# Seven small edits to a sparse attention and tanh-shrink kernel: crossbar turns for half of q, shared threshold biases, a deeper score pipeline, work moved to GpSimd

## The chip, the cores and the metric

One core of a Trainium2 chip. The metric is device microseconds of one execution, the median of several; a ratio is always the mean time of one kernel's fast runs over the mean time of the other's fast runs of the same rounds, so it is not quite the ratio of the medians quoted beside it. A difference between two edited kernels is the difference of their ratios times 552 us, the time of the kernel before; each ratio is known to about 0.15%, which is 0.8 us, so a difference of two is known to about 1 us. Stage lengths come from one profiled execution of each kernel.

## The reference

Eight batches of eight heads, 576 rows of 64. Scores are thresholded at the row's maximum less tau, then softmax; the result, 4608 rows of 512, goes through two matrices with h - tanh(h) between them.

```python
scores = scale * np.matmul(q, k.transpose(0, 1, 3, 2))
thresh = np.max(scores, axis=-1, keepdims=True) - tau
scores = np.where(scores >= thresh, scores, -1e9)
attn = softmax(scores)                      # cut
x = heads_side_by_side(np.matmul(attn, v))  # cut
h = x @ w_in
return (h - np.tanh(h)) @ w_out
```

## The kernel before

A turn is a transpose of a block of 128 columns, by TensorE into PSUM or by the crossbar, the transposing path of the DMA queue (`dma_start_transpose`), into SBUF. The depth is the number of slots by which the scores run ahead (`AHEAD`). In the views PE is TensorE, PEld its weight loads, DVE VectorE, ACT ScalarE, POOL GpSimd and SPq the DMA queue of SyncE.

Two heads make a pair; 32 pairs of nine tiles of 128 rows (kinds A, B, and M for the two heads' last 64 rows). Each tile goes through the engines slot by slot: TensorE scores, VectorE scale and row maximum (`sc`, `mx`), VectorE bias (`nb` = tau - max), ScalarE mask (`z`), a turn of the mask (`psZ` by TensorE in pairs 0 to 7, `zT` by the crossbar later), ScalarE exponential (`pT`), TensorE times v (`psO`). The hidden layer of the previous batch (`psH`, `psY`) is fed into the slots from pair 4 on. GpSimd splits the next pairs' q and k into high and low halves.

```python
NPE = 2 * HPAIR * TPP          # masks turned on TensorE: pairs 0 to 7
AHEAD = 7                      # scores run 7 slots ahead of the exponentials
MASK = 5                       # masks 5 slots ahead
zt_pool = pool("zt", 4)        # crossbar-turned masks in flight
ps_big = pool("ps_big", 2, space=PSUM)   # scores and turns of q, k
ps_y = pool("ps_y", 1, space=PSUM)       # turned masks, then output blocks
# ... cut ...
def split(p, t):                               # GpSimd
    x = hl_pool.tile([P, TPP, D], F32, name="xs", tag="xs")
    nc.gpsimd.tensor_scalar(out=x, in0=r, scalar1=QKSC, ...)
    nc.gpsimd.tensor_copy(out=hl[:, :, 0, :], in_=x)
    nc.gpsimd.tensor_tensor(out=hl[:, :, 1, :], in0=x, in1=hl[:, :, 0, :], op=ALU.subtract)

def turn(p, t):                                # nine 128x128 turns, one copy
    ps = ps_big.tile([P, W], FP16, name=f"ps_{t}", tag="big")
    for c in range(TPP): turn_chunk(...)
    nc.vector.tensor_copy(out=m, in_=ps)
# ... cut ...
def scores(i):
    # ... matmuls into ps ...
    mx = st_pool.tile([P, 1], F32, name="mx", tag="mx")
    nc.vector.tensor_scalar(out=sc, in0=ps[:, lo : lo + S], scalar1=SC, scalar2=None,
                            op0=ALU.mult, op1=ALU.max, accum_out=mx)

def shift(i):                                  # one bias for each tile
    nb = st_pool.tile([P, 1], F32, name="nb", tag="nb")
    nc.vector.tensor_scalar(out=nb, in0=mx, scalar1=-1.0, scalar2=tau,
                            op0=ALU.mult, op1=ALU.add)

def kink(i):                                   # the mask
    nc.scalar.activation(out=z, in_=sc, func=ACT.Prelu, bias=nb, scale=1.0, alpha=STEEP)
# ... cut ...
for s in range(-AHEAD, NTILE + LAG + 3):       # one slot
    shift(s + AHEAD - 1); scores(s + AHEAD)
    kink(s + MASK); bend(); weights(s)         # + hidden-layer steps
    attend(s - LAG)                            # + loads, splits, turns of later pairs
```

## Time and profile before

| | |
|---|---|
| time, median of 3 runs | 552.6 us (551.52 to 552.71) |
| span in the profile | 549.4 us, granted clock 0.999 |
| busy | TensorE 521.8, VectorE 444.1, ScalarE 443.3, GpSimd 286.5 us |

In a timeline or a table of stretches the first numbers are start and length in us. In a line of groups, the numbers after "x" and the count are total busy us and mean ns of one instruction; behind the second bar stands how long the engine was idle just before these instructions, and who ended most of that.

### The profile page before, as it was taken

The page shows a single profiled execution, that of the slowest core. Times are in us where ns is not written, and L with a number is a line of the kernel's source. Part 1 is how long each engine was busy: PE and PEld are TensorE (multiplying, and loading weights), DVE is VectorE, ACT ScalarE, POOL GpSimd, SP SyncE. Part 2 cuts the span into 40 slices and gives each one's busy share as a digit, 9 for nine tenths or more (in the row PEclk, how much of TensorE's full clock was granted, in tenths as well). Part 3 has the DMA queues.
Part 4 walks back from the last instruction along what each step waited for, and adds up shares of the span by engine and source line. Part 5 has one row for each costly group of instructions (what it writes and reads, how often), then busy time and mean ns, then how long its engine had stood idle before and what let it go on. Part 6 is the DMA issues. An engine that isn't in the chain of part 4 may idle for free.

```text
span 549.4 us, 13518 instructions
## 1 busy us (share of the span) xinstructions
PE 521.8 (95%) x4954; PEld 302.4 (55%) x4954; DVE 444.1 (81%) x1349; ACT 443.3 (81%) x640; POOL 286.5 (52%) x372
## 2 busy tenths in 40 slices
PE   5888999999999999999999999999999999999996
PEld 2566666665555555555555555555555555444442
DVE  5888988898988999898889898898989888544430
ACT  3999999899899898989888988989898989533320
POOL 6788977666556666556555655666665620000000
PEclk9999999999999999999999999999999999999999
DMA  6755644437879888889977798877878966310103
GB/s 168 216 183 146 205 125 145 128 74 157 161 153 172 178 181 160 169 171 170 186 174 173 165 182 164 167 180 179 163 169 171 185 87 144 66 39 38 40 38 78
DMA packets 183011, 80.33 MB, mean 146 GB/s; under 512 B 150688, under 2 KB 175264, under 8 KB 182944
## 3 DMA queue, kind: packets, MB, share of 16 engines
q1 hardware_dynamic: 182512, 79.17, 65.0%
q8 instruction: 39, 0.64, 0.5%
q10 hardware_dynamic: 432, 0.30, 0.2%
q14 instruction: 28, 0.23, 0.2%
HBM read 37.75 MB, written 9.44 MB: 86 GB/s over the span
## 4 chain that ended last, share of the span: by engine, by line
PE 72%; DVE 16%; ACT 8%; issue 2%; DMA 1%; SPq 0%; ACTq 0%; DVEq 0%
PE psY L470 20%; PE psH L444 18%; PE psS L292 15%; DVE sc L298 6%; PE psO L389 5%; ACT pT L352 4%; PE psS L282 3%; ACT z L324 3%; DVE g L463 3%; PE psHt L444 3%; PE ps_q L221 2%; PE ps_k L221 2%; PE psZ L343 2%; DVE yo L479 1%; DVE kT L233 1%
## 5 line engine op out<-in xcount | busy, mean ns | idle before, releaser
L298 DVE TENSOR_SCALAR_CACHE_REDUCE sc<-psS 128x576 f32<-128x576 f32 x288 | 216.3, 751 | 19.8 <-PE psS L282 12.5
L324 ACT ACTIVATE z<-sc,nb 128x576 bf16<-128x576 f32 x256 | 195.7, 769 | 14.3 <-DVE nb L307 13.4
L470 PE MATMUL psY<-w_out_sb,g 128*128 128x512 bf16 x576 | 145.4, 379 | 0.0
L360 ACT ACTIVATE pT<-zT 128x1152 f16<-128x1152 bf16 (+1 forms) x120 | 127.8, 1065 | 0.0
L444 PE MATMUL psH<-xT,w_in_sb 128*128 128x512 bf16 x480 | 124.0, 379 | 0.3
L292 PE MATMUL psS<-kT,qT 128*128 128x512 f16 (+1 forms) x512 | 105.2, 287 | 10.1 <-DVE nb L307 7.6
L292 PEld LDWEIGHTS <-qT 128*128 128x128 f16 x1024 | 75.5, 98 | 68.1 <-issue 15.9
L237 POOL COPY kS<-kT 64x1152 f16<-64x1152 f16 x31 | 35.3, 1140 | 141.4 <-DVE nb L307 141.4
L463 DVE SCALAR_TENSOR_TENSOR g<-th,psH 128x512 bf16<-128x512 f32 x128 | 87.4, 683 | 22.0 <-ACT th L457 22.0
L292 PE MATMUL psS<-kS,qT 128*128 128x512 f16 x496 | 101.4, 286 | 0.0
L457 ACT ACTIVATE th<-psH 128x512 f32<-128x512 f32 x128 | 74.7, 584 | 17.8 <-PE psH L444 17.6
L470 PEld LDWEIGHTS <-g 128*128 128x128 bf16 x576 | 49.6, 98 | 57.7 <-issue 2.6
L444 PEld LDWEIGHTS <-w_in_sb 128*128 128x128 bf16 x576 | 49.3, 98 | 55.0 <-issue 2.7
L389 PEld LDWEIGHTS <-pT 128*128 128x128 f16 x1280 | 55.6, 98 | 24.3 <-ACT pT L360 2.1
L389 PE MATMUL psO<-vb,pT 128*128 128x65 bf16 x1280 | 61.2, 193 | 0.6 <-ACT pT L360 0.6
L352 ACT ACTIVATE pT<-psZ 128x640 f16<-128x640 bf16 (+1 forms) x72 | 47.2, 656 | 6.9 <-PE psZ L343 6.2
L307 DVE TENSOR_SCALAR nb<-mx 128x1 f32<-128x1 f32 x288 | 42.6, 148 | 3.4
L324 ACT ACTIVATE zm<-sc,nb 128x576 bf16<-128x576 f32 x32 | 24.8, 774 | 23.1 <-DVE nb L307 23.1
L183 POOL TENSOR_TENSOR qhl<-xs,qhl 128x576 f16<-128x576 f32 x31 | 39.7, 1280 | 2.6
L183 POOL TENSOR_TENSOR khl<-xs,khl 128x576 f16<-128x576 f32 x31 | 39.7, 1279 | 2.6
L238 POOL COPY kS<-kT 64x1152 f16<-64x1152 f16 x31 | 35.4, 1142 | 1.3
L343 PE MATMUL psZ<-ident_bf,z 128*128 128x128 bf16 x288 | 26.5, 219 | 4.5 <-ACT pT L352 4.3
(72 smaller groups left out, 561.6 us busy)
## 6 DMA issues: line engine op xcount, KB each, us to landing
vraw<-in_v_dram SPq DMA_DIRECT2D x32, 256.0 KB, 3.5
out_dram<-yo SPq DMA_DIRECT2D x32, 256.0 KB, 2.6
kraw<-in_k_dram SPq DMA_DIRECT2D x31, 256.0 KB, 3.1
qraw<-in_q_dram SPq DMA_DIRECT2D x31, 256.0 KB, 3.2
wt<-in_moe_w_in_dram SPq DMA_DIRECT2D x8, 512.0 KB, 4.4
wt<-in_moe_w_out_dram SPq DMA_DIRECT2D x8, 512.0 KB, 3.9
vraw<-in_v_dram SPq DMA_DIRECT2D x64, 32.0 KB, 2.9
zT<-z SPq DMA_TRANSPOSE x96, 3.3
```

The lines of the kernel that those rows point to most:

```text
L183: nc.gpsimd.tensor_tensor(out=hl[:, :, 1, :], in0=x, in1=hl[:, :, 0, :], op=ALU.subtract)
L292: nc.tensor.matmul(out=ps[:, dst], lhsT=lhs, rhs=kk[:, src], start=(n == 0), stop=(n == 1),)
L298: nc.vector.tensor_scalar(out=sc, in0=ps[:, lo : lo + S], scalar1=SC, scalar2=None, op0=ALU.mult, op1=ALU.max, accum_out=mx,)
L307: nc.vector.tensor_scalar(out=nb, in0=mx, scalar1=-1.0, scalar2=tau, op0=ALU.mult, op1=ALU.add)
L324: nc.scalar.activation(out=z, in_=sc, func=ACT.Prelu, bias=nb, scale=1.0, alpha=STEEP)
L352: nc.scalar.activation(out=pt[:, off * P : (off + n) * P], in_=ps[:, 0 : n * P], func=ACT.Exp)
L360: nc.scalar.activation(out=pt[:, 0 : n * P], in_=zts.pop(i)[:, 0:n, :], func=ACT.Exp)
L389: nc.tensor.matmul(out=po[:, (j - 1 - 5 * hh) + ab, :], lhsT=pt[:, blk * P : (blk + 1) * P], rhs=vb[:, hh, c, :], start=(n == 0), stop=(n ...
L444: nc.tensor.matmul(out=ps, lhsT=w_in_sb[:, c, n * P : (n + 1) * P], rhs=xs[m][:, c, :] if m < B else xR[:, c, :, :], start=(c == 0), stop= ...
L457: nc.scalar.activation(out=th, in_=ps, func=ACT.Tanh)
L463: nc.vector.scalar_tensor_tensor(out=gs[m][:, n, :], in0=th, scalar=-1.0, in1=ps, op0=ALU.mult, op1=ALU.add,)
L470: nc.tensor.matmul(out=ps, lhsT=gs[m][:, n, ms * P : (ms + 1) * P], rhs=w_out_sb[:, n, :], start=(n == 0), stop=(n == DF_C - 1),)
```

## The change

Its intent: relieve TensorE, which is the bound from pair 8 on, by turning q of every second later pair and some masks of pairs 4 to 7 in the crossbar; save VectorE 128 tiny bias instructions by computing the biases of an A and a B tile together; give the pipeline one slot and the turned masks two buffers more; put part of the first split on GpSimd; shorten the tail.

```diff
-    NPE = 2 * HPAIR * TPP
+    def on_pe(i):
+        p, j = divmod(i, TPP)
+        return p < HPAIR or p < 2 * HPAIR and j in (0, 1, 4, 5, 6)
-    AHEAD = 7
+    AHEAD = 8
-    zt_pool = pool("zt", 4)
+    zt_pool = pool("zt", 6)
 # split: x in place; split_first, second half: three GpSimd instructions
 # in place of one on ScalarE and one on VectorE, issued before the loop
+    def q_by_dma(p):
+        return p >= 2 * HPAIR and p % 2 == 1
     def turn(p, t):
+        if t == "q" and q_by_dma(p):
+            nc.sync.dma_start_transpose(out=m..., in_=hl...)
+            return
     def scores(i):
-        mx = st_pool.tile([P, 1], F32, name="mx", tag="mx")
+        if kind(j) == "B":
+            mx = mxs[i] = mxs.pop(i - 1)
+        else:
+            mx = mxs[i] = st_pool.tile([P, 2], F32, name="mx", tag="mx")
     def shift(i):
+        if kd == "A":
+            return
+        n = 2 if kd == "B" else 1
         nc.vector.tensor_scalar(
-            out=nb, in0=mx, scalar1=-1.0, scalar2=tau, op0=ALU.mult, op1=ALU.add
+            out=nb[:, 0:n], in0=mx[:, 0:n], scalar1=-1.0, scalar2=tau,
+            op0=ALU.mult, op1=ALU.add,
         )
     def weights(i):
-            ps = ps_y.tile([P, 5 * P], BF16, name="psZ", tag="y")
+            pl, tag = (ps_h, "h") if i % 2 and i < HPAIR * TPP else (ps_y, "y")
+            ps = pl.tile([P, 5 * P], BF16, name="psZ", tag=tag)
 # v: last rows loaded once, GpSimd writes both copies
 # layers: three quarters of an output block one stage earlier,
 # the last block in two halves of 256 columns, stored from two queues
 # (cut: order of the first masks, slots in which turns and hidden-layer steps
# are issued, where the rows of a crossbar-turned q lie, one-time constants)
```

## The prediction

> **What bounds the kernel now.** I read the page first (TensorE busy 95% of 549.4 us, VectorE and ScalarE 81% each, the clock full throughout), then cut the span where the work changes and read the busy times stage by stage. Columns: stretch, length, busy us (instructions) of PE, PEld, DVE, ACT, POOL, granted clock, DMA share, GB/s.
>
> ```profile
> 0.00:9.20 9.20, 3.13 (x25) 2.02 (x26) 2.98 (x24) 3.63 (x7) 4.17 (x17) 1.00 0.64 174
> 9.20:20.30 11.10, 9.40 (x83) 5.23 (x82) 10.17 (x31) 7.45 (x12) 8.60 (x11) 1.00 0.76 226
> 20.30:68.80 48.50, 43.10 (x595) 31.38 (x595) 42.50 (x144) 45.86 (x74) 43.58 (x54) 1.00 0.57 175
> 68.80:127.50 58.70, 54.85 (x655) 36.41 (x652) 51.09 (x163) 53.71 (x88) 42.72 (x54) 1.00 0.42 119
> 127.50:472.80 345.30, 340.63 (x3258) 195.04 (x3257) 309.10 (x950) 308.79 (x422) 187.44 (x240) 1.00 0.82 166
> 472.80:544.80 72.00, 70.69 (x347) 32.28 (x345) 28.25 (x44) 23.23 (x39) 0.00 (x0) 1.00 0.13 45
> 544.80:549.40 4.60, 0.00 (x0) 0.00 (x0) 0.00 (x0) 0.59 (x1) 0.00 (x0) 0.83 0.25 57
> ```
>
> Seven stages, three kinds of limit. From 127.5 us to 544.8 us TensorE is busy 98.6% and 98.2%: it is the bound, and only less work on it, or fewer holes in it, helps. Between 20.3 and 127.5 us (head pairs 1 to 8 by their first score tile) no engine is full: four engines stand at 86 to 95% and wait for each other. The ends, 9.2 us before the first scaled score and 4.6 us after the last matmul, are latency.
>
> A busy TensorE need not be a full one, so I looked at starts in the timeline. This is the second stage of that kind, pairs 1 to 4, around the q turn of a pair:
>
> ```profile
> 39.86 0.60 ACT L352 ACTIVATE pT<-psZ 128x512 f16<-128x512 bf16 x1 [0.52 <-PE psZ L343]
> 39.99 0.41 PE L292 MATMUL psS<-kT,qT 128*128 128x512 f16 x2 [0.55 <-DVE nb L307]
> ...
> 40.51 0.44 PE L343 MATMUL psZ<-ident_bf,z 128*128 128x128 bf16 x5
> ...
> 41.09 0.67 PE L221 MATMUL ps_q<-ident_f,qhl 128*128 128x128 f16 x9
> ...
> 41.80 0.76 DVE L233 COPY qT<-ps_q 128x1152 f16<-128x1152 f16 x1 [0.22 <-PE ps_q L221]
> ```
>
> ScalarE waits for the turned mask (psZ, one buffer, so a turn must wait for the exponential before it), TensorE waits for VectorE to release a score buffer, VectorE waits for the q turn. A ring of three engines, none full. Summing starts in 20.3 to 68.8 us, I find about 9 us of holes on TensorE: 5.4 behind the score matmuls, 3.9 behind psZ. In a later period of four pairs (231.3 to 290.4 us, 59.17 us; the pattern repeats to 0.1 us), psY and psH matmuls start every 216 ns, and I find only 1.4 us of holes, 0.7 of it in the four slots that have no hidden-layer work.
>
> These groups give the unit costs:
>
> ```profile
> L307 DVE TENSOR_SCALAR nb<-mx 128x1 f32<-128x1 f32 x288 | 42.6, 148 | 3.4
> L233 DVE COPY qT<-ps_q 128x1152 f16<-128x1152 f16 x31 | 23.4, 756 | 7.7 <-PE ps_q L221 7.7
> L343 PE MATMUL psZ<-ident_bf,z 128*128 128x128 bf16 x288 | 26.5, 219 | 4.5 <-ACT pT L352 4.3
> L221 PE MATMUL ps_q<-ident_f,qhl 128*128 128x128 f16 x288 | 21.8, 220 | 0.5 <-DVE sc L298 0.3 <-DVE nb L307 0.2
> ```
>
> Finally the waits of the DMA queue on SyncE, and the transposes' landing:
>
> ```profile
> SPq L332 <- ACT pT L360: 64.1, 37, 3.9
> ```
>
> ```profile
> zT<-z SPq DMA_TRANSPOSE x96, 3.3
> ```
>
> 37 transposes stand in the queue until an exponential gives a turned tile back: four such tiles are too few. It costs nothing yet: from issue to the exponential I count 4.06 us at least, 7.4 in the median, and the exponentials from turned tiles have 0.0 us of idle before them.
>
> **What the Trainium skill says.** "TensorE: Matmul & The Clock Gate", "Wait — 56ns, not 53.3ns?": warm matmuls of 128 columns start 55.6 ns apart, of 512 columns 215.7 ns. The trace agrees: nine turns take 0.67 us (8 x 55.6 + 220), and the long matmuls start 216 ns apart. So a turn of 128 columns is worth 56 ns, not the 220 ns of its row. "VectorE: DVE Perf Modes", "The three transpose paths": a crossbar transpose lands in SBUF, a TensorE one in PSUM; here the PSUM route costs the 756 ns copy as well. "Perfetto Trace Analysis", "Identifying the Most-Contended Engine": matmul busy share is no measure of headroom, and DMA occupancy misleads with 16 engines. I therefore judge the DMA side (0.82 busy) by landings against deadlines, not by its share. Same page, "Matmuls": independent groups should rotate through PSUM banks, which is what the second psZ buffer does; the psZ waits agree.
>
> **The change, part by part.**
> 1. q of pairs 9, 11, ..., 31 by crossbar: 12 pairs x 9 turns x 55.6 ns = 6.0 us off TensorE, all in the TensorE-bound stage. 12 copies x about 0.67 us start to start (8.0 us) off VectorE, 12 fewer claims on the two big PSUM buffers. It adds 12 transposes of 1.3 us issue to SyncE; the second copy of v's last rows, 31 later issues of about 0.6 us, is gone, so the queue is not longer. In the period I measured, packets take 51.4 us of the 16 engines; 18 more blocks of 128 packets at 24 ns add 3.5, the lost v rows give 0.8 back: about 54 of 58 us. Six turned tiles let transposes start up to 3.9 us earlier. Holes: I take 0.3 us off each of about six periods. Together -7.5 us (6.0 + 1.8, rounded down).
> 2. In pairs 4 to 7, 16 of 36 mask tiles (j = 2, 3, 7, 8) go by crossbar: 4 x 2 x 9 turns x 55.6 ns = 4.0 us off TensorE, and eight fewer exponentials on ScalarE (1150 against 596 + 704 ns). Start sums for this stage give floors near 52 us for TensorE, 51 for ScalarE, 53 for VectorE of 58.7. After: about 48, 51, 51. With the ring slackened by parts 2 and 3, I expect 54: -4.5 us.
> 3. Threshold biases: one instruction for tiles A and B, 160 in place of 288. 128 x 148 ns = 19 us in the rows, but these overlap: start to start about 60 to 110 ns each, so some 10 us of VectorE, none of it on the path of the TensorE-bound stage. In pairs 1 to 4 it works with the alternating psZ buffer. Floors there: VectorE 43 to about 41.5, ScalarE 43.6, but GpSimd about 45.6 (9.1 us a pair plus nine 1.0 us weight casts). GpSimd is the new limit: 48.5 becomes 46: -2.5 us.
> 4. Start: the second half of the first split moves to GpSimd, earlier; VectorE loses 1.3 us of split in a stretch where it is 92% busy, and the first masks, at 13.5 us now, can come before 12. GpSimd gets about 2.6 us more before the next pair's split. -1.5 us.
> 5. The deeper pipeline: one more slot with scores but no weights at the start, one with weights but no scores at the end: +0.5 us.
> 6. Tail: three quarters of an output block (2.6 us) move from the tail into the period that starts at pair 8, TensorE-bound in both places: 0. The last block in two halves: a copy of 256 columns in place of the 0.59 us one, the last two stores on two queues in place of two issues in a row: -1.0 us.
> 7. Split in place and the v rows' source: memory and traffic, about 0.
>
> Sum: -7.5 - 4.5 - 2.5 - 1.5 + 0.5 - 1.0 = -16.5 us. 552.6 - 16.5 = **536 us**.
>
> **The rivals.** (a) The crossbar becomes the bound. For it: windows of 13.7 and 16.1 us already show shares of 0.94 and 0.93, one exponential came 4.06 us after its issue, and landings reach 4.6 us. Against: no exponential waits today, and the buffers that held transposes back are added. If so, parts 1 and 2 give back most: 543 to 550 us. (b) GpSimd paces the first 127 us: it is 90% busy in pairs 1 to 4 and gets more at the start; then the swapped k comes late and parts 2 to 4 give 3 us rather than 8.5: 541 us. (c) The ring opens more than I think and the holes of the TensorE stage close too (4.2 us of score waits over all periods): 529 us. (d) VectorE takes over from TensorE: it needs about 54.5 us of a 59.2 us period by starts, about 51.5 after, against 57.5 to 58 for TensorE: unlikely.
>
> **Range and chances.** The certain part is turns removed from a full TensorE (6 us); the early stages are guesses about a ring and carry most of the spread; (a) makes the slow side longer. 8 times in 10 between **529 and 544 us**. Faster by 2% means under 541.5 us: **0.79**; within 2% **0.19**; slower **0.02**.
>
> **What would show it.** Right: a period of four pairs of about 58 us in place of 59.17 (the one from pair 8 longer by 2.6 us), 180 turns fewer on TensorE (108 of q, 72 of psZ), 160 bias instructions, the queue's wait for the exponentials nearly gone, exponentials still without idle time, pairs 1 to 4 near 46 us with GpSimd the fullest, first masks before 12 us, 3.6 us after the last matmul. Wrong: idle time before the exponentials from turned tiles or before scores that wait for q (rival a), score matmuls waiting for the swapped k (rival b), or a period that stays at 59 us although the turns are gone.

## The result, and the profile after

The changed kernel takes 545.05 us (544.2 to 545.15, 4 runs), the kernel before 552.06 us on the same chip: ratio 0.9872, 95% interval 0.9851 to 0.9893. That is 7.0 us, where 16.5 us were predicted; 545.05 us lies outside the range of 529 to 544 us. It is 1.3% faster, within the 2% that count as the same, to which the prediction gave 0.19.

To see where, I cut the span by work done rather than by the clock: at the first scaled score, at the end of attention of pairs 0, 3, 7 and 31 (the start of the reciprocal of the pair's second head), and at the last matmul. The last column is a kernel from the experiments below, with one part of the change mended.

| stage, us | before | after | with two narrow biases |
|---|---|---|---|
| to the first scaled score | 9.2 | 8.5 | 9.3 |
| to the end of pair 0 | 22.9 | 22.5 | 21.3 |
| pairs 1 to 3 | 36.1 | 36.4 | 34.7 |
| pairs 4 to 7 | 58.7 | 56.8 | 56.2 |
| pairs 8 to 31 | 347.7 | 347.1 | 343.5 |
| tail to the last matmul | 70.2 | 67.7 | 67.7 |
| after it | 4.6 | 3.9 | 3.9 |

The first rows are rough: the first scaled score comes between 8.5 and 9.5 us in profiles of kernels that start alike. The tail is as predicted (2.6 us of it now lie in the stage of pairs 8 to 31). The loss is in the middle: pairs 1 to 3 gained nothing, and pairs 8 to 31, where 6 us of turns left a full TensorE and 2.6 us of output block came in, gained 0.6 us, where they should have gained about 4.9. These are the middle stretches of the changed kernel; columns as in the prediction's table (the tail is cut at 539.2 us, 0.1 us behind the last matmul).

```profile
31.06:67.42 36.36, 31.43 (x450) 23.05 (x448) 34.50 (x97) 34.41 (x57) 34.54 (x42) 1.00 0.61 184
67.42:124.20 56.78, 49.05 (x562) 31.43 (x570) 52.81 (x144) 52.85 (x80) 43.17 (x54) 1.00 0.77 165
124.20:471.32 347.12, 337.29 (x3135) 188.97 (x3188) 309.97 (x851) 308.79 (x424) 186.66 (x239) 1.00 0.88 173
471.32:539.20 67.88, 66.66 (x323) 31.80 (x329) 26.93 (x42) 22.41 (x38) 0.00 (x0) 1.00 0.14 44
```

TensorE is busy less while the stage is as long, and VectorE, which lost over a hundred instructions, is as busy as before (in the stage of pairs 8 to 31: 309.97 us; before, 311 us by the same cut) or, in pairs 1 to 3, busier (34.50 against 32.1 us). Note that this trace lacks 68 matmul records of 4790 (the weight loads, 4790, are complete), all of the hidden layer, one about every 6 us, so its TensorE busy time is a little low. The groups say what became of VectorE:

```profile
L337 DVE TENSOR_SCALAR nb<-mx 128x2 f32<-128x2 f32 x128 | 44.4, 347 | 2.5
L337 DVE TENSOR_SCALAR nb<-mx 128x1 f32<-128x1 f32 x32 | 4.6, 144 | 0.0
L357 ACT ACTIVATE z<-sc,nb 128x576 bf16<-128x576 f32 x256 | 194.2, 771 | 21.9 <-DVE nb L337 21.3
L394 ACT ACTIVATE pT<-zT 128x1152 f16<-128x1152 bf16 x104 | 119.9, 1153 | 0.0
L227 PE MATMUL ps_q<-ident_f,qhl 128*128 128x128 f16 x180 | 14.0, 223 | 1.5 <-POOL qhl L180 1.1 <-DVE sc L323 0.3
```

The bias of one column takes 144 ns, as all 288 did before (148 ns). The bias of two columns takes 347 ns in the mean. 160 instructions now cost VectorE 49.1 us where 288 cost 42.6. ScalarE's masks wait 21.3 us for a bias, but that is no loss: in the kernel before they waited 13.4 us (A and B tiles) and 23.1 us (M tiles). The exponentials from turned tiles wait for nothing (0.0), and TensorE waited for a q turned by the crossbar once, 1.5 us, so the crossbar is not what holds the kernel back, and 108 of 288 q turns are gone, as planned. One long bias, in the timeline of all engines:

```profile
216.29 0.41 PE L313 MATMUL psS<-kT,qT 128*128 128x512 f16 x2
216.32 1.28 POOL L180 TENSOR_TENSOR qhl<-qraw,qhl 128x576 f16<-128x576 f32 x1
216.47 0.08 DVE L323 DVE_READ_ACCUMULATOR sc<-psS 128x1 f32 x1
216.54 0.41 PE L313 MATMUL psS<-kS,qT 128*128 128x512 f16 x2
216.56 0.60 ACT L491 ACTIVATE th<-psH 128x512 f32<-128x512 f32 x1
216.59 1.03 DVE L337 TENSOR_SCALAR nb<-mx 128x2 f32<-128x2 f32 x1
...
217.05 1.16 ACT L394 ACTIVATE pT<-zT 128x1152 f16<-128x1152 bf16 x1
...
217.54 0.74 DVE L323 TENSOR_SCALAR_CACHE_REDUCE sc<-psS 128x576 f32<-128x576 f32 x1
```

GpSimd starts a subtraction at 216.32 that ends at 217.60. VectorE starts its bias at 216.59; it ends at 217.62. The next scaled score, which frees a PSUM buffer for TensorE, can only start at 217.54, although its scores were complete at 216.95. Of the 57 two-column biases over 250 ns in this trace, all 57 end within 40 ns of the end of a GpSimd instruction (28 of them of a subtraction); of the 42 that start while GpSimd is idle, none is over 170 ns. The wait does not show as idle time of VectorE, since it lies inside the instruction's own record.

That became theory W: **a bias of more than one column waits until the GpSimd instruction in flight is done**. The Trainium skill has this on a page that I had not read for the prediction, "SBUF — State Buffer", "Who interferes with whom": VectorE's second pair of SBUF ports is GpSimd's only pair; a tensor_scalar can enter a 2-port mode, and then whoever comes second fully blocks for the whole instruction of the other. Its rivals: R, the missing gain lies in the ring of the early stages and in the crossbar, and the long biases are a symptom; later, D, the eighth slot costs in itself.

### The profile page after: what moved, and what is told of

Its sections match the earlier page's. It is cut to its first block, busy times and chain, and to the rows that moved or that the text cites. A ratio compares the mean times of both kernels' runs of the same rounds, so it can differ in the third digit from the quotient of the medians.

```text
span 542.9 us, 12962 instructions
## 1 busy us (share of the span) xinstructions
PE 507.5 (93%) x4722; PEld 290.3 (53%) x4790; DVE 447.1 (82%) x1196; ACT 439.3 (81%) x630; POOL 290.7 (54%) x390
## 4 chain that ended last, share of the span: by engine, by line
PE 67%; DVE 19%; POOL 6%; ACT 4%; issue 3%; DMA 0%; ACTq 0%; SPq 0%; DVEq 0%; POOLq 0%
PE psY L504 19%; PE psH L478 17%; PE psS L313 14%; DVE sc L323 9%; PE psO L423 5%; DVE g L497 3%; PE psS L303 3%; PE ps_k L227 3%; PE psHt L478 3%; DVE nb L337 2%; ACT z L357 2%; DVE osb L438 1%; POOL kS L256 1%; PE ps_q L227 1%; PE psO L412 1%
## 5 line engine op out<-in xcount | busy, mean ns | idle before, releaser
L357 ACT ACTIVATE z<-sc,nb 128x576 bf16<-128x576 f32 x256 | 194.2, 771 | 21.9 <-DVE nb L337 21.3
L504 PE MATMUL psY<-w_out_sb,g 128*128 128x512 bf16 (+1 forms) x556 | 138.4, 373 | 2.2 <-issue 0.8
L394 ACT ACTIVATE pT<-zT 128x1152 f16<-128x1152 bf16 (+1 forms) x128 | 137.3, 1073 | 0.0
L478 PE MATMUL psH<-xT,w_in_sb 128*128 128x512 bf16 x451 | 118.0, 379 | 6.5 <-DVE g L497 4.4
L337 DVE TENSOR_SCALAR nb<-mx 128x2 f32<-128x2 f32 (+1 forms) x160 | 49.1, 307 | 2.5
L386 ACT ACTIVATE pT<-psZ 128x640 f16<-128x640 bf16 (+1 forms) x56 | 37.6, 671 | 5.1 <-PE psZ L377 5.0
L180 POOL TENSOR_TENSOR qhl<-qraw,qhl 128x576 f16<-128x576 f32 x31 | 39.7, 1281 | 2.6
L180 POOL TENSOR_TENSOR khl<-kraw,khl 128x576 f16<-128x576 f32 x31 | 39.7, 1281 | 2.6
L250 DVE COPY kT<-ps_k 128x1152 f16<-128x1152 f16 x31 | 23.4, 756 | 13.6 <-PE ps_k L227 13.2
L514 DVE COPY yo<-psY 128x512 f32<-128x512 f32 (+1 forms) x31 | 21.1, 679 | 11.3 <-PE psY L504 6.4
L438 DVE TENSOR_TENSOR osb<-psO,rc 128x256 bf16<-128x256 f32 x64 | 27.2, 424 | 2.2
```

The lines of the kernel that those rows point to most:

```text
L337: nc.vector.tensor_scalar(out=nb[:, 0:n], in0=mx[:, 0:n], scalar1=-1.0, scalar2=tau, op0=ALU.mult, op1=ALU.add,)
L394: nc.scalar.activation(out=pt[:, 0 : n * P], in_=zts.pop(i)[:, 0:n, :], func=ACT.Exp)
L478: nc.tensor.matmul(out=ps, lhsT=w_in_sb[:, c, n * P : (n + 1) * P], rhs=xs[m][:, c, :] if m < B else xR[:, c, :, :], start=(c == 0), stop= ...
L504: nc.tensor.matmul(out=ps, lhsT=gs[m][:, n, ms * P : (ms + 1) * P], rhs=w_out_sb[:, n, cols], start=(n == 0), stop=(n == DF_C - 1),)
```

## The experiments

All are correct. Each call also timed the kernel before on its chip (551.3 to 552.0 us). "Narrow" below means the changed kernel with two one-column biases (bias_two_narrow), 539.21 us, ratio 0.9771.

| run | median us | ratio to before | 95% interval |
|---|---|---|---|
| the change itself | 545.05 | 0.9872 | 0.9851 to 0.9893 |
| bias_strided | 545.05 | 0.9881 | 0.9866 to 0.9895 |
| bias_two_narrow | 539.21 | 0.9771 | 0.9757 to 0.9786 |
| bias_three_columns | 544.41 | 0.9867 | 0.9853 to 0.9881 |
| wide_bias_short_gpsimd | 543.34 | 0.9843 | 0.9829 to 0.9857 |
| before_deeper | 558.18 | 1.0116 | 1.0099 to 1.0133 |
| before_deeper_wide_bias | 560.97 | 1.0165 | 1.0150 to 1.0180 |
| per_tile_bias_8 | 540.53 | 0.9797 | 0.9783 to 0.9811 |
| per_tile_bias_7 | 540.33 | 0.9798 | 0.9785 to 0.9812 |
| narrow_q_on_tensore | 548.70 | 0.9950 | 0.9936 to 0.9963 |
| narrow_q_on_tensore_7 | 546.50 | 0.9906 | 0.9893 to 0.9920 |
| narrow_masks_on_tensore | 541.05 | 0.9814 | 0.9800 to 0.9827 |
| narrow_one_psz | 542.28 | 0.9834 | 0.9821 to 0.9847 |
| narrow_first_split_old | 539.62 | 0.9778 | 0.9765 to 0.9791 |
| narrow_q_all_crossbar | 537.83 | 0.9751 | 0.9728 to 0.9775 |

**1. The pair's bias as two narrow instructions.**

```diff
-        nc.vector.tensor_scalar(out=nb[:, 0:n], in0=mx[:, 0:n], ...)
+        for c in range(n):
+            nc.vector.tensor_scalar(out=nb[:, c : c + 1], in0=mx[:, c : c + 1], ...)
```

> The changed kernel with the pair's bias as two one-column instructions at the same place in the program, 288 in all again. Theory W: all at 140-160 ns, time 538-542 us, no more than 1.5 us above the strided one although 128 instructions come back. Rival R: 545-547 us, since VectorE gets 128 instructions more.

539.21 us: 5.6 us below the change (0.0101 of ratio), with 128 instructions more. The groups of this run:

```profile
L338 DVE TENSOR_SCALAR nb<-mx 128x1 f32<-128x1 f32 x288 | 35.7, 148 | 0.0
L358 ACT ACTIVATE z<-sc,nb 128x576 bf16<-128x576 f32 x256 | 194.0, 771 | 18.9 <-DVE nb L338 18.7
```

All are 142 to 156 ns whatever GpSimd does. Rival R falls. The masks' wait for the bias hardly shrinks (21.3 to 18.7 us), so that wait was not the cost. The cost is that VectorE, held by the bias, comes late to what TensorE waits for: the scaled score that frees a score buffer, and the hidden layer's `g`. TensorE's waits, first in the change, then in this run:

```profile
PE psS L313 <- DVE sc L323: 9.2, 20, 0.8
PE psH L478 <- DVE g L497: 4.4, 7, 0.8
```

```profile
PE psS L313 <- DVE sc L323: 4.8, 12, 0.8
PE psH L479 <- DVE g L498: 2.3, 7, 0.4
```

In pairs 8 to 31 alone TensorE's waits for a scaled score, for `g` and for `xT` fall from 5.8 to 2.4 us (6.0 us in the trace of the next run, which has the wide bias and lacks no record); the stage itself is 3.6 us shorter. Another 1.6 us of the gain lie in pairs 1 to 3.

**2. The same two columns, two elements apart.**

```diff
-    out=nb[:, 0:n], in0=mx[:, 0:n]
+    out=nb[:, 0 : 2 * n - 1 : 2], in0=mx[:, 0 : 2 * n - 1 : 2]   # tiles [P, 4]
```

> The changed kernel with one edit: the two maxima and two biases of an A/B pair lie two elements apart, so the bias is still one VectorE instruction with two columns, but not two adjacent ones. Theory W (the two-column bias on adjacent fp32 columns runs in a mode that must wait until the GpSimd instruction in flight is done: in the changed kernel its row is 347 ns in the mean and up to 1032 ns, and a long one ends when a GpSimd instruction ends): the 128 two-column biases fall to 150-170 ns each with none over 250, TensorE's waits for the score buffers shrink, and the time falls from 545.0 to 537-541 us. Rival R (the missing gain lies in the ring of the early stages and in the crossbar, the long biases are only a symptom of idle time): the rows stay long, or get short and the time stays at 544-546 us.

```profile
L337 DVE TENSOR_SCALAR nb<-mx 128x2 f32<-128x2 f32 x128 | 44.7, 349 | 2.5
```

No effect on row or time. (The longest row of the change was 1274 ns; 1032 is that of the example above.) My reading that adjacency opens the mode was wrong; the wait stays, and so does the time, which fits the cause if not the condition.

**3. Three columns.**

```diff
-    out=nb[:, 0:n], in0=mx[:, 0:n]
+    out=nb[:, 0 : 2 * n - 1], in0=mx[:, 0 : 2 * n - 1]   # third column always zero
```

> The changed kernel, with the pair's bias as one instruction over three adjacent columns, the third a zero column that nothing uses (so an odd count). Theory M (the wait for GpSimd comes with a mode that is entered when the count of columns is even; the strided pair had the same count and the same wait): the 128 biases are 145-170 ns each, none over 250, and the time is that of two narrow biases or a little less, 537.5-539.5 us. Rival T (any bias of more than one column waits for GpSimd): mean near 300 ns again, time 544-546 us.

```profile
L345 DVE TENSOR_SCALAR nb<-mx 128x3 f32<-128x3 f32 x128 | 45.0, 351 | 2.5
```

An odd count waits as well: theory M falls, its rival T holds. "VectorE: DVE Perf Modes", "What auto-detection actually checks", gives the condition of the 2-port mode for a single source and a destination in SBUF as outermost non-unit dims "both even or equal"; a stride of two, and three columns on both sides, meet it. All three forms agree with that page. No run has a bias of several columns outside that mode, so that it is the mode, and not just more than one column, is the page's account and not shown here.

**4. The wide bias kept, GpSimd's subtraction cut in three.**

```diff
-    nc.gpsimd.tensor_tensor(out=hl[:, :, 1, :], in0=x, in1=hl[:, :, 0, :], op=ALU.subtract)
+    for cs in (slice(0, 3), slice(3, 6), slice(6, TPP)):
+        nc.gpsimd.tensor_tensor(out=hl[:, cs, 1, :], in0=x[:, cs, :], ...)
```

> The changed kernel, its adjacent two-column bias as it is, but GpSimd's subtraction in the split of q and k (1281 ns, the instruction behind most long biases) cut into three of three chunks each, some 450 ns. Theory W2 (a bias of more than one column cannot start until the GpSimd instruction in flight is done, so the wait is as long as what is left of that instruction): biases that start during a subtraction fall from 550 ns in the mean to about 250, none of them over 650; the mean of all two-column biases falls from 347 to 240-270 ns, and 1.5-3 us of the 5.8 us come back: 542-543.5 us. If the wait is for something else, such as a queue of GpSimd's work as a whole: rows and time as before, 544.5-546 us (GpSimd gets more instructions).

```profile
L181 POOL TENSOR_TENSOR qhl<-qraw,qhl 128x192 f16<-128x192 f32 x93 | 48.6, 549 | 2.6
L339 DVE TENSOR_SCALAR nb<-mx 128x2 f32<-128x2 f32 x128 | 38.1, 298 | 2.5
```

GpSimd does more in all, yet the wide biases shorten and 1.6 us come back (ratio 0.9872 to 0.9843, intervals that just overlap). In the profile pairs 8 to 31 take 344.1 in place of 347.1 us, nearly the 343.5 us of the narrow biases, while the head up to the end of pair 0 is 1.6 us longer. Biases that start during a subtraction fall from 599 to 372 ns in the mean (33 and 34 of them; the 550 ns of the expectation does not come out of the trace), the longest from 1274 to 551 ns, which is just the length of a piece. The pieces took 549 ns, not the 450 I had assumed, so the two means (372 and 298 ns) miss what I wrote (about 250, and 240 to 270). All 64 long ones again end with a GpSimd instruction. This is theory W by intervention and not only by coincidence in time.

**5. The eighth slot alone, and with the wide bias, in the kernel before.**

```diff
-    AHEAD = 7
+    AHEAD = 8
```

> The kernel before with the scores one slot further ahead and nothing else (the base of the next run). By my step for the deeper pipeline +0.5 us: 552-553.5 us; both theories the same.

> The kernel before, one slot further ahead, and the shared two-column bias (adjacent columns) of the change alone. Theory W: the two-column biases at 300-350 ns in the mean, long ones where GpSimd is at work, time 2 to 6 us above the run without them (554-559 us). Rival R: 160 short biases, time 0 to 2 us below it.

The slot alone costs 6.4 us (I had +0.5); the wide bias on top another 2.7 us, with a mean of 311 ns. The second confirms W; the first was a surprise. The cost is even, 0.83 us in each period of four pairs (60.00 against 59.17 us), plus 1.4 us to the end of pair 0. TensorE's idle time before the first score matmuls in the two kernels, before and deeper:

```profile
L292 PE MATMUL psS<-kT,qT 128*128 128x512 f16 x256 | 97.6, 381 | 10.1 <-DVE nb L307 7.6 <-DVE sc L298 1.1
```

```profile
L292 PE MATMUL psS<-kT,qT 128*128 128x512 f16 x256 | 97.3, 380 | 13.3 <-DVE sc L298 13.1
```

With the slots shifted by one against the turns, TensorE waits longer for VectorE to release a score buffer (by starts, about 1.0 us of holes in a period that were not there before). In pairs 8 to 31 these waits are 7.6 us, 3.3 of them right behind a q turn and the rest 4 to 5 us after one.

**6. One bias per tile again, at depth 8 and at depth 7** (diff: `shift` and the tiles of `mx` as in the kernel before; then AHEAD = 7).

> The changed kernel with the bias of every tile by itself in the slot after its scores, as in the kernel before; scores still 8 slots ahead. Theory W (the two-column bias waits for GpSimd; that is all that was wrong with part 3 of the change): as with two narrow biases, 538-540.5 us. Theory P (placing both biases at the B tile also holds the mask of the A tile back): 536-538 us, and ScalarE's wait for the bias, 18.7 us with two narrow ones, falls under 5 us.

> The same with the scores 7 slots ahead, as in the kernel before. Theory D (the eighth slot costs in itself, since it moves the turns of the next pair onto other slots; alone in the kernel before it cost 6.3 us, 0.83 us in each period of four pairs): 3 to 6 us under the run with 8 slots, 532-536 us. Rival (in the changed kernel the eighth slot costs nothing, since half of the q turns are gone and the shared biases need it): within 1.5 us of the run with 8 slots.

0.9797 and 0.9798: in the changed kernel the eighth slot costs nothing. Theory D falls, and so does P: a bias in the tile's own slot is 1.4 us slower than both at the B tile (about the noise), not faster, and ScalarE's wait for it does not fall either: at depth 7 it is 9.6 us for the A and B tiles but 27.7 us for the M tiles, where two narrow biases have 18.7 and 0.0 us. The first, profiled execution of the run at depth 8 took 1839 us, with matmuls of 128x512 at 1059 to 1095 ns in the mean; its other four executions took 539.85 to 540.8 us. Its output-block matmuls start 840 ns apart in the median, where 216 is usual, although its recorded clock is 1.0. I leave it out as slow and cannot say what it was.

**7. q on TensorE, at depth 8 and 7.**

```diff
-        return p >= 2 * HPAIR and p % 2 == 1
+        return False
```

> The kernel of the run with two narrow biases (539.2 us), with q of all pairs turned on TensorE again. My step 1 has -7.5 us for the crossbar, so 545.2-547 us if it holds (period 57.9 to 58.9-59.2 us). If the crossbar's traffic gives part of it back: under 543 us.

> The changed kernel with one bias per tile, scores 7 slots ahead and q of all pairs on TensorE. Theory X (the eighth slot costs some 6 us only while every q is turned on TensorE, since it puts the q turn where the scores behind it must wait for a big PSUM buffer; the crossbar takes that wait away, so my step 1 and my step for the deeper pipeline belong together): 543-545.5 us, that is 3.5-5.5 us under the 548.7 us of q on TensorE with 8 slots. Rival (the crossbar is worth 9-10 us whatever the depth): 549-551 us.

At depth 7 the crossbar is worth 6.0 us (0.9906 against 0.9798 for the same kernel with the crossbar), as much as the 12 x 9 x 55.6 ns of TensorE time. At depth 8 it is worth 9.9 us (0.9950 against 0.9771; 9.6 of it in pairs 8 to 31). With all q on TensorE the kernel of depth 8 is 2.4 us slower than that of depth 7; theory X has the right sign, but I expected 3.5 to 5.5. The two also differ in where the biases stand, which with the crossbar made the deeper one 1.5 us faster, so the eighth slot by itself may cost up to 3.9 us here; with half of q in the crossbar it costs nothing. No run changes the depth alone with all q on TensorE in the changed kernel.

**8. Masks of pairs 4 to 7 on TensorE** (diff: `return p < 2 * HPAIR` in `on_pe`).

> The kernel of the run with two narrow biases (539.2 us), with all masks of pairs 4 to 7 turned on TensorE, as in the kernel before. My step 2 has -4.5 us, so 543-544.5 us if it holds. If the freed TensorE time was only turned into other waits in that stage, 539-541 us.

+2.4 us, and the profile has 2.2 of it in pairs 4 to 7 (58.4 against 56.2 us). The part works, at half the size I gave it, between my two expectations.

**9. One psZ buffer** (diff: `pl, tag = ps_y, "y"`).

> Two narrow biases, and the turned masks of pairs 0 to 3 all in the one psZ buffer, as in the kernel before. My step 3 has -2.5 us for that stage: 540.5-541.5 us (539.2 without the edit; 538.7 on the chip of the last call) if the second buffer is what helped there. If GpSimd or the score buffers hold the stage anyway, within 0.8 us of the unedited one.

+3.5 us, more than the 2.5 I gave; the profiled execution, 2.6 us longer, has 2.0 of it in pairs 1 to 3. ScalarE's exponentials wait longer for the turned mask, first the narrow kernel, then this one:

```profile
L387 ACT ACTIVATE pT<-psZ 128x640 f16<-128x640 bf16 x32 | 22.7, 710 | 3.5 <-PE psZ L378 3.4
```

```profile
L387 ACT ACTIVATE pT<-psZ 128x640 f16<-128x640 bf16 x32 | 22.5, 704 | 6.0 <-PE psZ L378 6.0
```

**10. The first split at its old place** (diff: the ScalarE and VectorE instructions of the kernel before, inside the loop).

> Two narrow biases, and the second half of the first split back on ScalarE and VectorE at its old place. My step 4 has -1.5 us: 540.2-541.2 us if it holds; no slower than without the edit if GpSimd's extra 2.6 us at the start cost as much as they saved.

+0.4 us, within the noise. The profile shows the head up to the end of pair 0 1.25 us longer (the first mask at 13.8 in place of 11.8 us) and pairs 4 to 7 0.4 us shorter. That makes 0.9 us between the two profiled executions and 0.4 us between the means: a gain of 1.5 us is not shown, and neither is where the rest went.

**11. q of all pairs from 8 on by crossbar** (diff: `return p >= 2 * HPAIR`).

> Two narrow biases, and q of every pair from 8 on by crossbar, 24 in place of 12. If the crossbar still has room, as my step 1 argued from landings against deadlines: another 12 x 0.5 us off TensorE, 533-535 us (539.2 without the edit). If it is near its end (my rival a; the DMA share of that stage is 0.91 already): idle time before the exponentials from turned tiles or before scores that wait for q, and 540 us or more.

Another 6 us left TensorE, and 1.1 us were gained (0.9751 against 0.9771, intervals overlap). The six executions fall into two groups: the first two took 541.15 and 541.42 us, the other four 537.31 to 538.09 us. The waits of the first one, the only one profiled:

```profile
PEld L313 <- DMA qT<-qhl: 11.4, 8, 2.7
...
PE psS L313 <- DMA qT<-qhl: 7.8, 7, 2.2
```

Neither expectation: it is no slower, but in this execution TensorE stands 7.8 us before scores that wait for a turned q, once in nearly every period, and exponentials stand 0.7 us before turned masks. With every second pair TensorE did so for 1.5 us (the change) and 0.3 us (narrow). So my rival (a) shows, one step further than the change goes; whether the four faster executions had these waits is not known.

Every kernel without the wide bias and with half or all of the later q in the crossbar beats both the one before and the changed one. Clearly over 2% faster than the kernel before are three: two narrow biases (539.21 us), those with the first split at its old place (539.62 us), and those with q of all later pairs in the crossbar (537.83 us); they are not clearly different from each other.

## Why the prediction was wrong, point by point

- **The step that failed is part 3**, the shared bias: "160 in place of 288 ... some 10 us of VectorE, none of it on the path". I costed a two-column instruction as a one-column one. It takes 347 ns instead of 148, because it waits for GpSimd, and it holds VectorE in front of the scores that TensorE waits for. Instead of a small gain it costs 5.6 us against two narrow instructions. With narrow biases in its place 12.6 us are gained, and 539.2 us is inside the range. I had also called VectorE far from the bound (rival d): as a sum it was, but one engine late by up to 1 us at the wrong moment is enough.
- **Part 1, q by crossbar, -7.5 us.** The 6.0 us of turns are what the crossbar was worth at depth 7 (6.0, known to about 1 us), so the 1.8 us for fewer holes did not show there. At depth 8 with narrow biases the period is 57.9 us against 59.17; 1.0 of that is work, and the other 0.27 us is about the 0.3 that I gave for holes. With the wide bias it was 58.26, close to the "about 58" that I asked for as proof, which shows how weak that test was.
- **Part 2, masks of pairs 4 to 7, -4.5 us:** the 4.0 us of TensorE turns are gone, but the stage is a ring of engines and not TensorE-bound; measured 2.4 us. With narrow biases ScalarE is the fullest there, 53.1 of 56.2 us. I had said so myself and still counted the work nearly one for one.
- **Part 3's second half, the second psZ buffer, -2.5 us:** right in kind, measured 3.5 us. That GpSimd would then pace pairs 1 to 3 (rival b) was not shown: in the changed kernel three engines stand level there, at 34.4 to 34.5 of 36.4 us, one of them VectorE with its waiting biases. Narrow biases took 1.6 us off that stage, so GpSimd's 34.5 us were not its floor; with them GpSimd is busy 32.9 of 34.7 us, level with ScalarE (33.1), and no run tells what limits the stage then.
- **Part 4, the start, -1.5 us:** 1.25 us at the head, 0.4 us in all, which is within the noise.
- **Part 5, the eighth slot, +0.5 us:** by itself 6.4 us in the kernel before, 2.4 to 3.9 us in the changed one with q on TensorE, nothing with the crossbar. The estimate came out near the right size by luck, because part 1 removes a cost that I had not seen.
- **Part 6, the tail, -1.0 us:** 0.7 us (4.6 to 3.9 us after the last matmul, read from the profiles; no run has it alone).
- **Sum:** 6.0 + 2.4 + 3.5 + 0.4 from single edits and 0.7 from the profiles = 13.0 us, against 12.6 measured for the kernel with narrow biases; with the 5.6 us of the wide bias, 7.0, as measured. The parts are not strictly additive (q is worth 6.0 or 9.9 us by depth), so this closes to a microsecond or two and no better.
- **Rival (a)** was not what happened: with half of q in the crossbar exponentials from turned tiles never waited, and scores waited for a turned q once, 1.5 us.
- A sign that I named and that did not come: the queue's waits put down to exponentials did not go; they rose from 64.1 to 90.2 us, with six turned tiles in place of four. So buffer shortage was not their cause, or not the only one. No run settles what those waits are; they cost no exponential anything.
- Two readings of the prediction do not hold as written. Four engines at 86 to 95% is true of the stretch from 20.3 to 68.8 us; from there to 127.5 us GpSimd is busy 42.72 of 58.70 us, which is 73%. And the landings of at most 4.6 us are those of a stretch of 22 us; over the whole kernel before they reach 5.5 us.

## What to carry to other kernels

Before merging tiny VectorE instructions, ask whether the merged one reads and writes SBUF with more than one element a partition while GpSimd is at work: then it can wait a whole GpSimd instruction, and the wait is booked as its own duration, not as idle time. Compare the mean of one instruction, not the count, and try the narrow form first. And when a stage is a ring of engines that wait for each other, do not count work taken off one of them at its full length: here 4.0 us of turns were worth 2.4 us, while 6.0 us off a nearly full TensorE were worth 6.0 us at depth 7 and 9.9 us at depth 8, and the next 6.0 us only 1.1 us.

## What the Trainium skill lacked or had wrong

- "SBUF — State Buffer" has the mechanism, and the runs agree (57 of 57 long biases end with a GpSimd instruction). It gives no example this small: here an instruction of two elements a partition pays it, 347 ns in the mean and up to 1274 ns against 148 ns, and that a profile shows the wait inside the instruction's record, with no idle time before it.
- "VectorE: DVE Perf Modes" advises, for chained operations, to minimize their count. Here 160 instead of 288 was 5.6 us slower, because of the wait for GpSimd. Its condition for the 2-port mode held in all three forms tried (two adjacent columns, two with a stride, three).
- No page gives the room of the crossbar beside other traffic. Here TensorE waited 1.5 us (the change) and 0.3 us (narrow) for 12 turned q, and 7.8 us for 24 in the one profiled execution, at DMA shares of 0.88, 0.91 and 0.94 in the stage of pairs 8 to 31.
- No page gives the cause of a single execution of 1839 us among others of 540 us, with 512-column matmuls 840 ns apart where 216 ns is usual and a recorded clock of 1.0. It belongs to "TensorE: Matmul & The Clock Gate", "Seeing it yourself", whose caveats on the recorded clock come nearest but have no execution of this length.
